# Second-layer weights with eight neighbouring rows on a partition, and ScalarE writing the first layer's result in that order

## The chip, the cores and the metric

The kernel runs on one core of a Trainium2 chip. The metric is the device time of one execution in microseconds, taken as the median of several runs. Five engines matter here: TensorE (PE, with its weight loads as PEld), VectorE (DVE), ScalarE (ACT), GpSimd (POOL) and SyncE (SP). The last two also start most of the DMA transfers.

## What is computed

A linear attention with cosine weights over 8 batches of 576 tokens is followed by a mixture of experts with one expert per token. The change is in the experts, whose core is

```python
def _moe_ref(x, w_gate, w_output_gate, w1, w2):          # x: 4608 x 512
    e_idx = np.argmax(x @ w_gate, axis=1)                # 8 experts
    ...
    for e in range(E):
        mask = e_idx == e
        h = np.maximum(x[mask] @ w1[e], 0.0)             # w1[e]: 512 x 1024
        ye = h @ w2[e]                                   # w2[e]: 1024 x 512
        out[mask] = gate_w[mask, None] * eom[mask, e, None] * ye
```

The weights are float32 in memory; the kernel turns them into float16 while they are loaded.

## The kernel before

The program has two stages that overlap a little. Up to about 159 us the attention is computed batch by batch in 36 units (a batch and a pair of token chunks), whose finished rows are scattered, sorted by expert, into a buffer in memory (`xs`). From then on the experts' work is done in tiles of 128 sorted rows, 39 of them in the main loop, numbered j.

The order of instructions on each engine is the order in which the code is written. A tile passes through these steps: `fetch(j)` loads its rows from `xs`; `x_tr(j)` transposes them on TensorE (tile `xtsp`) and ScalarE copies the result out (`xts`, line 801); `layer1(j)` runs 8 matmuls of 512 columns into `hp`, 1024 float32 values on each partition (line 836), and ScalarE takes the positive part of them and writes it as float16 into `hs` (line 845, for tile 0 in two halves, line 848); `h_tr(j)` transposes `hs` in 8 blocks of 128 columns, on TensorE (line 818) with a VectorE copy into `hts` (line 820), or, for the tiles 18 to 36 (`BY_DMA`), by a DMA transpose that SyncE starts (line 813); `layer2(j)` runs 8 matmuls of 512 columns into `yp` (line 868), VectorE scales the result, and GpSimd scatters it into the output (line 879).

In the main loop TensorE's order for a tile outside `BY_DMA` is

```python
            if j < NMAIN and j - 1 not in BY_DMA:
                h_tr(j - 1)
            if j + 1 < NMAIN:
                x_tr(j + 1)
            ...
                layer1(j)
            ...
                    layer2(m)      # m = j - 1; m = j - 2 where m is in BY_DMA
```

so that the 8 matmuls of one `layer2` stand between the end of `layer1(j)` and the first transpose of `hs(j)`.

The weights of the 8 experts are loaded by GpSimd in order of rank, two DMAs for each: `load_w(r, 0)` brings the first layer (line 238), `load_w(r, 1)` the second (line 241). They are started between the scatters of rows and of results, all on GpSimd's one DMA queue. ScalarE waits on the semaphores of the loads (`wsem`) ahead of the copy of line 801.

Of the kernel before, what the change touches and what calls it, by code (L numbers as in the profile page):

```python
# [17 lines left out]
AF = mybir.ActivationFunctionType  # L18
# [4 lines left out]
def kernel(  # L23
# [13 lines left out]
    ACT = nc.scalar  # L37
# [191 lines left out]
    def load_w(r, m):  # L229

        if r not in wreg:
            wreg[r] = GP.value_load(ordi[0:1, r:r + 1], min_val=0, max_val=E - 1)
            if r > 1:

                GP.wait_ge(wsem[r % 2], 16 * (r % 2) + 32 * (r // 2))
        er = wreg[r]
        if m == 0:
            d = GP.dma_start(w1v[:, r], moe_w1[bass.ds(er, 1)].rearrange(
                "o (c p) f -> p (o c) f", p=128))
        else:  # L240
            d = GP.dma_start(w2v[:, r], moe_w2[bass.ds(er, 1)].rearrange(
                "o (c p) d2 -> p (o c) d2", p=128))
        d.then_inc(wsem[r % 2], 16)
        tc.declare_no_dep(d.ins, group="mm", reason="ranks loaded before")
        tc.add_to_no_dep_group("w", d.ins)
# [28 lines left out]
    if True:  # L274
# [488 lines left out]
        def tcol(m, j):  # L763
            tab, jj = (tabs[0], j) if j < EARLY else (tabs[1], j - EARLY)
            return tab[jj:jj + 1, m:m + 1]
# [56 lines left out]
        def layer1(j, hp_t=None):  # L822
            ev = PE.value_load(tcol(2, j), min_val=0, max_val=7)
            evr[j] = ev
            xts = xtss.pop(j)
            hs = fsb.tile([P, F], F16, name=f"hs{j}", tag="hs", bufs=3)
            hss[j] = hs
            if hp_t is None:
                hp_t = pqo.tile([P, 4, 256], F32, name=f"hp{j}", tag="qo")
                hp = hp_t[:].rearrange("p a w -> p (a w)")  # L830
                hps = [hp[:, 0:512], hp[:, 512:1024]]
            else:
                hp, hps = None, [x[:] for x in hp_t]
            for fh in range(2):
                for kc in range(4):
                    mm = PE.matmul(hps[fh], xts[:, kc, :],  # L836
                                   wt[:, bass.ds(ev, 1),
                                      kc * F + fh * 512:kc * F + fh * 512 + 512],
                                   start=(kc == 0), stop=(kc == 3))
                    tc.declare_no_dep(mm.ins, group="w", reason="waits on wsem")  # L840
                    tc.add_to_no_dep_group("mm", mm.ins)
                    if j < 2:
                        tc.declare_no_dep(mm.ins, group="att", reason="is of rank 0 or 1")
            if hp is not None:
                ACT.activation(hs[:], hp, AF.Relu)  # L845
            else:
                for fh in range(2):
                    ACT.activation(hs[:, fh * 512:fh * 512 + 512], hps[fh], AF.Relu)

        spare = {}  # L850

# [131 lines left out]
        for i, (b, c) in enumerate(units):  # L983
# [86 lines left out]
            for w in wload.get(i, ()):  # L1070
                load_w(*w)
# [5 lines left out]
        rows = []  # L1077
        q_out(*outs[0], late=rows)
        layer1(0, kv_tiles("hp"))
        x_tr(2)  # L1080
        layer1(1)
        h_tr(0)
        next(first_half, None)
        scatter(NG - 1, 0)
        scatter(NG - 1, 1)
        q_out(*outs[1], late=rows)
        load_w(3, 1)
        layer1(2)
        h_tr(1)
        x_tr(3)  # L1090
# [16 lines left out]
        next(late)  # L1107
        layer2(2)
        load_w(4, 1)
        for j in range(4, NMAIN + 1):  # L1110
            if j < NMAIN and j - 1 not in BY_DMA:
# [67 lines left out]
```

## Time and profile before

| | us |
|---|---|
| median of 3 runs | 329.62 |
| the three runs | 331.42, 329.14, 329.62 |
| profiled execution, its own time | 331.24 |
| its span from the first to the last instruction | 329.4 |

The profile is of one execution. Its time is 1.84 us longer than its span. TensorE has a matmul under way in 284.5 us of the span (86%), VectorE is busy for 179.0 us, ScalarE for 176.7 us and GpSimd for 134.0 us. Each expert's first-layer weights are 512 rows of 4 KB in memory, the second-layer weights 1024 rows of 2 KB; half as many bytes arrive on chip, because they are turned into float16 on the way.

### The profile page before, as it was taken

How to read it: one execution, taken by the hardware profiler on the slowest of the kernel's cores; microseconds unless marked ns; L12 is line 12 of the kernel's file. 1: busy time of each engine (PE TensorE's matmuls, PEld its weight loads, DVE VectorE, ACT ScalarE, POOL GpSimd, SP SyncE). 2: the span in 40 equal slices, each digit the busy share in tenths (PEclk: the TensorE clock that was granted, in tenths of full speed). 3: DMA queues.
4: the chain of work that ended last, by engine and by line, in shares of the span. 5: the costliest groups of instructions: out<-in, count | busy, mean ns of one | idle time of the engine just before them, and what ended most of it. 6: DMA issues, size and time to landing. Idle time of an engine off the chain costs nothing. (4 is left out here: it accounts for less than half of the span.)

```text
span 329.4 us, 10190 instructions
## 1 busy us (share of the span) xinstructions
PE 284.5 (86%) x3624; PEld 180.3 (55%) x3624; DVE 179.0 (54%) x534; ACT 176.7 (54%) x346; POOL 134.0 (41%) x169
## 2 busy tenths in 40 slices
PE   6888898997887769787982989999999999999990
PEld 2566687775776557654541455555554444444440
DVE  7347688877989987967681633333322222322240
ACT  4488899887787658835620323333345344444410
POOL 8002224358625676388267343252221322232231
PEclk9999999999999989979998799999999999999997
DMA  7999779686956899999977999999948867785711
GB/s 245 339 385 334 188 241 310 209 288 245 315 170 216 242 241 259 220 221 252 217 123 223 159 232 234 233 240 255 284 89 196 184 169 190 176 183 137 193 46 46
DMA packets 58208, 71.87 MB, mean 218 GB/s; under 512 B 23406, under 2 KB 38318, under 8 KB 58160
## 3 DMA queue, kind: packets, MB, share of 16 engines
q0 software_dynamic: 17552, 31.05, 42.5%
q1 hardware_dynamic: 40608, 40.17, 41.6%
q8 instruction: 32, 0.52, 0.7%
q14 instruction: 16, 0.13, 0.1%
HBM read 67.61 MB, written 16.17 MB: 254 GB/s over the span
## 5 line engine op out<-in xcount | busy, mean ns | idle before, releaser
L868 PE MATMUL yp<-wt,hts 128*128 x312 | 75.1, 385 | 6.7 <-issue 6.7
L836 PE MATMUL hp<-wt,xts 128*128 x304 | 71.8, 379 | 0.5 <-issue 0.4
L536 POOL TENSOR_TENSOR xr<-wt,rc 128x512 f16<-128x512 f32 x33 | 37.3, 1139 | 61.6 <-DVE rc L547 53.7
L845 ACT ACTIVATE hs<-hp 128x1024 f16<-128x1024 f32 x38 | 38.9, 1023 | 39.7 <-PE hp L836 39.7
L875 DVE TENSOR_SCALAR ysp<-yp,xg 128x512 f32<-128x512 f32 x24 | 18.0, 751 | 69.0 <-PE yp L868 69.0
L868 PEld LDWEIGHTS <-hts 128*128 128x128 f16 x312 | 30.7, 99 | 43.9 <-issue 8.8
L521 PE MATMUL qo<-kvm,wt 64*64 64x162 f32 x1024 | 44.3, 304 | 9.8 <-DVE rc L546 5.1
L801 ACT COPY xts<-xtsp 128x512 f16<-128x512 f16 x39 | 22.7, 586 | 51.0 <-PE xtsp L785 37.3
L526 ACT ACTIVATE wt<-qo,cosq 128x324 f32<-128x324 f32 x72 | 36.0, 531 | 23.4 <-PE qo L521 18.1
L528 DVE SCALAR_TENSOR_TENSOR wt<-qo,sinq,wt 128x324 f32<-128x324 f32 x72 | 37.3, 550 | 19.9 <-ACT wt L526 16.3
L836 PEld LDWEIGHTS <-xts 128*128 128x128 f16 x312 | 29.1, 98 | 29.3 <-issue 1.3
L384 PE MATMUL kvp<-wt 64*64 64x132 f32 x1152 | 40.6, 278 | 4.7 <-issue 1.9
L521 PEld LDWEIGHTS qo<-kvm,wt 64*64 64x64 f32 x1024 | 35.1, 133 | 14.8 <-DVE wt L528 6.3
L384 PEld LDWEIGHTS kvp<-wt 64*64 64x64 f32 x1152 | 32.5, 132 | 9.9 <-issue 5.2
L879 POOL DMA_INDIRECT out_dram<-ysp,sidx x17 | 16.7, 985 | 48.3 <-DVE sidx L805 40.3
L336 ACT ACTIVATE wt<-wt,tanc 128x256 f32<-128x256 f32 x63 | 28.5, 516 | 0.0
L875 DVE TENSOR_SCALAR ysb<-yp,xg 128x512 f32<-128x512 f32 x15 | 11.3, 751 | 28.9 <-PE yp L868 26.8
L342 DVE TENSOR_SCALAR wt<-wt,cosc 128x256 f32<-128x256 f32 x63 | 24.4, 434 | 0.0
L498 PE MATMUL qtp<-ident,qr 128*128 128x128 f32 x128 | 21.8, 295 | 1.5 <-ACT qr L486 1.0
L879 POOL DMA_INDIRECT out_dram<-ysb,sidx x11 | 10.8, 984 | 28.2 <-DVE ysb L875 16.7
L486 ACT ACTIVATE qr<-wt 128x512 f32<-128x512 f32 x32 | 20.6, 648 | 0.0
L501 ACT COPY wt<-qtp 128x512 f32<-128x512 f32 x32 | 18.9, 591 | 1.6 <-PE qtp L498 1.1
(274 smaller groups left out, 322.7 us busy)
## 6 DMA issues: line engine op xcount, KB each, us to landing
wt<-in_moe_w_dram POOLq DMA_DIRECT2D x16, 1024.0 KB
wt<-in_k_dram SPq DMA_DIRECT2D x16, 576.0 KB
wt<-in_v_dram SPq DMA_DIRECT2D x16, 576.0 KB
wt<-in_q_dram SPq DMA_DIRECT2D x16, 576.0 KB
xg<-xs SPq DMA_DIRECT2D x43, 129.0 KB
xs<-zt SPq DMA_DIRECT2D x9, 129.0 KB
hts<-hs SPq DMA_TRANSPOSE x19
out_dram<-ysp,sidx POOLq DMA_INDIRECT x17
```

The lines of the kernel that those rows point to most:

```text
L336: d = ACT.activation(tvs[:, c, :, 1:65], vbuf[b % 2][:, :, c, :], AF.Copy, scale=tanc[:, c:c + 1])
L342: DVE.tensor_scalar(kcs[:, :, c, :], kbuf[b % 2][:, :, c, :], cosc[:, c:c + 1], 0.0, ALU.mult, ALU.max)
L384: mm = PE.matmul(outs(i, mp), kcs[rows, m, c, :], mov, start=first, stop=(c == NCH - 1), skip_group_check=True)
L521: PE.matmul(qo[64 * l:64 * l + 64, 2 * mp + ih, 0:162], qT[r, hf, ih, l, :], kvms[b if c < 4 else b - 1 + l][r, n0:n0 + 2, :], start=True, ...
L526: d0 = ACT.activation(t, qo[:, :, 0:81], AF.Copy, scale=cosq[:, c:c + 1])
L528: d1 = DVE.scalar_tensor_tensor(u[:, h0:h0 + 4, :], qo[:, :, 81:162], sinq[:, c:c + 1], t, ALU.mult, ALU.add)
L536: e.tensor_tensor(xrows[:, slot + x, 0:DM].bitcast(F16).rearrange("p (h d) -> p h d", d=D), u[:, 8 * x:8 * x + 8, 0:64], rc[:, 8 * x:8 * x ...
L836: mm = PE.matmul(hps[fh], xts[:, kc, :], wt[:, bass.ds(ev, 1), kc * F + fh * 512:kc * F + fh * 512 + 512], start=(kc == 0), stop=(kc == 3))
L845: ACT.activation(hs[:], hp, AF.Relu)
L868: mm = PE.matmul(yp, hts[:, fc, :], wt[:, bass.ds(ev, 1), 4 * F + fc * DM:4 * F + fc * DM + DM], start=(fc == 0), stop=(fc == 7))
L875: DVE.tensor_scalar(ysb, yp, xg[:, DM + 2:DM + 4].bitcast(F32), None, ALU.mult)
L879: d = GP.indirect_dma_start(out=out[:, :], out_offset=bass.IndirectOffsetOnAxis(ap=idx, axis=0), in_=ysb, in_offset=None, bounds_check=N - ...
```

## The change

Before, partition p gets the rows p, 128 + p, 256 + p, ... of the second-layer weights: eight pieces of 2 KB from eight places. Afterwards it gets the rows 8p to 8p + 7, which are neighbours: 16 KB from one place. The second layer then multiplies, in its step c, the features 8p + c instead of 128c + p. So the 128 columns of block c of `hs` must hold the features c, 8 + c, 16 + c, ..., and ScalarE reads every eighth value of `hp` for each block: its input steps by 32 bytes through the accumulator memory (PSUM), where it read neighbours before. Its output is written in order as before. For tile 0 each half writes 64 columns of each block.

```diff
         else:
             d = GP.dma_start(w2v[:, r], moe_w2[bass.ds(er, 1)].rearrange(
-                "o (c p) d2 -> p (o c) d2", p=128))
+                "o (p c) d2 -> p (o c) d2", p=128))
...
+            hv = hs[:].rearrange("p (c q) -> p c q", c=8)
             if hp is not None:
-                ACT.activation(hs[:], hp, AF.Relu)
+                ACT.activation(hv, hp.rearrange("p (q c) -> p c q", c=8), AF.Relu)
             else:
                 for fh in range(2):
-                    ACT.activation(hs[:, fh * 512:fh * 512 + 512], hps[fh], AF.Relu)
+                    ACT.activation(hv[:, :, fh * 64:fh * 64 + 64],
+                                   hps[fh].rearrange("p (q c) -> p c q", c=8), AF.Relu)
```

No instruction moves. On GpSimd, around the load of the first expert's second-layer weights, the program of before has this order (`xs` are scattered rows, `xr` the rows in the making, 128x8x512 the shape of the load):

```order
L238 DMA wt<-in_moe_w_dram 128x4x1024
L633 DMA xs<-xr_1014,di@1_0_1852 36992x516
L536 TENSOR_TENSOR xr_1643<-wt,rc_4_2082 128x512
L633 DMA xs<-xr_1014,di@1_0_1852 36992x516
L536 TENSOR_TENSOR xr_1643<-wt,rc_4_2082 128x512
L241 DMA wt<-in_moe_w_dram 128x8x512
```

The changed program has the same order there:

```order
L238 DMA wt<-in_moe_w_dram 128x4x1024
L633 DMA xs<-xr_1014,di@1_0_1852 36992x516
L536 TENSOR_TENSOR xr_1643<-wt,rc_4_2082 128x512
L633 DMA xs<-xr_1014,di@1_0_1852 36992x516
L536 TENSOR_TENSOR xr_1643<-wt,rc_4_2082 128x512
L241 DMA wt<-in_moe_w_dram 128x4096
```

Only the shape of the load differs: one run of 4096 values for a partition in place of eight runs of 512.

## Rows read from the trace of the kernel before

**Rows 1.** Busy time by stretch: engines, granted clock, DMA share, GB/s.

```profile
core 0: us, PE busy (x) PEld busy (x) DVE busy (x) ACT busy (x) POOL busy (x), PEclk, DMA share, GB/s
200.00:210.00 10.00, 10.00 (x65) 5.30 (x64) 3.44 (x7) 3.80 (x5) 4.79 (x5) 1.00 1.16 233
260.00:280.00 20.00, 20.00 (x110) 9.69 (x109) 4.37 (x10) 9.06 (x11) 4.99 (x6) 1.00 0.73 180
```

**Rows 2.** Timeline of PE, 199 to 213 us: start, us, what.

```profile
201.47 1.89 PE L868 MATMUL yp<-wt,hts 128*128 x8
203.20 0.61 PE L818 MATMUL htsp<-ident,hs 128*128 128x128 f16 x8
203.64 0.39 PE L785 MATMUL xtsp<-ident,xg 128*128 128x128 f16 x4
203.87 1.89 PE L836 MATMUL hp<-wt,xts 128*128 x8
205.59 1.89 PE L868 MATMUL yp<-wt,hts 128*128 x8
207.32 0.61 PE L818 MATMUL htsp<-ident,hs 128*128 128x128 f16 x8
```

**Rows 3.** Timeline of ACT, the same stretch.

```profile
201.67 1.02 ACT L845 ACTIVATE hs<-hp 128x1024 f16<-128x1024 f32 x1 [1.06 <-PE hp L836]
204.14 0.58 ACT L801 COPY xts<-xtsp 128x512 f16<-128x512 f16 x1 [1.45 <-PE xtsp L785]
205.79 1.02 ACT L845 ACTIVATE hs<-hp 128x1024 f16<-128x1024 f32 x1 [1.06 <-PE hp L836]
```

**Rows 4.** Timeline of PE's weight loads, 206 to 209 us.

```profile
207.11 0.65 PEld L818 LDWEIGHTS <-hs 128*128 128x128 f16 x8
```

**Rows 5.** Timeline of all engines, 183.5 to 185.4 us.

```profile
183.85 1.03 ACT L845 ACTIVATE hs<-hp 128x1024 f16<-128x1024 f32 x1
184.93 0.10 PEld L818 LDWEIGHTS <-hs 128*128 128x128 f16 x1 [0.34 <-ACT hs L845]
```

**Rows 6.** Groups by line and shape: count, busy us, mean ns, idle before.

```profile
L845 ACT ACTIVATE hs<-hp 128x1024 f16<-128x1024 f32 x38 | 38.9, 1023 | 39.7 <-PE hp L836 39.7
L848 ACT ACTIVATE hs<-kvphp 128x512 f16<-128x512 f32 x2 | 1.1, 593 | 0.0
L558 DVE TENSOR_REDUCE glog<-gl 128x32 f32<-128x256 f32 x16 | 9.5, 592 | 0.5
L558 DVE TENSOR_REDUCE glog<-gl 128x16 f32<-128x128 f32 x4 | 1.5, 368 | 0.1
```

**Rows 7.** Line 581, a reduction over neighbouring values: ns minimum/median/maximum.

```profile
L581 DVE TENSOR_REDUCE ei@0_0_1056<-oh@0_0_1053 x1: 230/230/230, 57.4 to 57.4; 128x9 f32<-128x72 f32 x1
...
L581 DVE TENSOR_REDUCE ei@3_0_2764<-oh@3_0_2761 x1: 186/186/186, 145.2 to 145.2; 128x4 f32<-128x32 f32 x1
```

**Rows 8.** Line 845 from 183.8 to 243 us.

```profile
L845 ACT ACTIVATE hs<-hp x14: 1023/1023/1030, 183.9 to 239.0; 128x1024 f16<-128x1024 f32 x14
```

**Rows 9.** Timeline of ACT, 310 to 321.5 us: the last two tiles.

```profile
311.49 1.02 ACT L845 ACTIVATE hs<-hp 128x1024 f16<-128x1024 f32 x1 [1.09 <-PE hp L836]
315.44 1.02 ACT L845 ACTIVATE hs<-hp 128x1024 f16<-128x1024 f32 x1 [2.93 <-PE hp L836]
```

**Rows 10.** Who waited for whom, PE's weight loads, 184 to 322 us.

```profile
PEld L868 <- DMA hts<-hs: 0.2, 1, 0.2
```

**Rows 11.** DMA packets from 207 to 209 us: a second-layer load fills the queue.

```profile
DMA packets 408, 0.42 MB, mean 211 GB/s; under 512 B 2, under 2 KB 406, under 8 KB 408
```

**Rows 12.** DMA packets from 213 to 215 us: a first-layer load fills the queue.

```profile
DMA packets 210, 0.43 MB, mean 215 GB/s; under 512 B 2, under 2 KB 2, under 8 KB 210
```

**Rows 13.** The weights in memory: who starts their loads, and who waited.

```profile
L238 POOL DMA_DIRECT2D wt<-in_moe_w_dram x8: 798/806/837, 109.4 to 213.6; - x8
...
L241 POOL DMA_DIRECT2D wt<-in_moe_w_dram x8: 952/974/1000, 116.4 to 217.9; - x8
...
  ACT xts L801: 1.4, 1
```

**Rows 14.** Timeline of ACT, 223 to 232 us, around that one wait.

```profile
224.92 0.58 ACT L801 COPY xts<-xtsp 128x512 f16<-128x512 f16 x1 [1.45 <-PE xtsp L785]
...
229.04 0.59 ACT L801 COPY xts<-xtsp 128x512 f16<-128x512 f16 x1 [1.45 <-DMA wt<-in_moe_w_dram]
```

**Rows 15.** Waits of POOL and then of PE, 100 to 160 us: total, times, longest.

```profile
POOL xr L536 <- DMA xs<-xr,di@1_0_1852: 7.7, 1, 7.7
...
PE qo L521 <- DVE wt L528: 5.1, 6, 1.8
PE qo L521 <- DVE rc L546: 3.1, 2, 1.7
```

## The prediction

> **What bounds the kernel now.** I began with the busy time by stretch. [...] The view of the chain that ended last holds two pieces here, both in the last 8 us, and is of no use. Next came the timelines of PE and ACT side by side for one tile. Outside the DMA-transposed tiles, TensorE's period is 4.12 us (first transpose of `hs` at 203.20, the next at 207.32) [rows 2], and inside it ScalarE's step on `hs` starts at 205.79 and lasts 1.02 us [rows 3]. The reader is to see how narrow the gap is. The weight load of the first transpose starts at 207.11 [rows 4]. The one place where it had to wait for `hs` shows the delay between the two: the step ended at 183.85 + 1.03 = 184.88, the load started at 184.93 [rows 5], 0.05 us later. So the slack is 207.11 - (205.79 + 1.02) - 0.05 = 0.25 us a tile. All that ScalarE's step grows beyond that, TensorE waits for.
>
> **What the load gains.** Both loads already run near one rate. In 2 us in which a second-layer load fills the queue, 408 packets bring 0.42 MB, 211 GB/s, nearly all of them the 1 KB that a 2 KB row becomes [rows 11]; in 2 us of a first-layer load, whose pieces are twice as long, 210 packets bring 0.43 MB, 215 GB/s [rows 12]. A piece twice as long was worth 2%. A load of 1 MB takes some 5.0 us at 211 GB/s, so 0.1 us each if eight-fold pieces gain as much again as two-fold ones did, and 0.3 us if each doubling does (three doublings, 6%). For the four loads of ranks 0 to 3, which go out while attention and the first tiles run, that is 0.4 to 1.2 us. On GpSimd the start of a second-layer load takes 0.97 us against 0.81 for a first-layer load with half the pieces [rows 13]; with an eighth of the pieces I expect it below 0.81, eight times 0.2 to 0.3 us, beside TensorE's work.
>
> Who would notice? In the experts' stage nobody: the one wait ended by a weight load is the copy at 229.04, and it was idle for 1.45 us before it, exactly as the copy at 224.92 was while waiting for TensorE [rows 14], so the load landed as the transposes did. In the attention, GpSimd waited once, 7.7 us, for scattered rows that stand in the same queue behind weight loads, and TensorE waited for VectorE for 5.1 and 3.1 us in that stretch [rows 15]. One second-layer load, of rank 0, lies ahead of those rows; so 0.1 to 0.3 us of that wait can go. I take -0.3 us for all of this. The other bound is a loss: a piece eight times as long holds a DMA engine eight times as long, and the query loads and instruction fetches that share the engines wait behind it. The trace shows no such piece in a queue of weights. I allow up to +1 us there, a fifth of the 5 us for which one weight load holds the engines, and use it for the range only.
>
> **What ScalarE's step costs.** No row shows ScalarE reading PSUM with a step. So I bound it. Below: the cost is nothing; the step stays at 1023 ns [rows 6]. A gain has no source, since the number of values, the output and the count of instructions are the same. Above: the nearest row is VectorE's reduction of line 558, which reads float32 values 64 bytes apart (in SBUF, not PSUM). 256 values take 592 ns and 128 take 368 [rows 6], so 224/128 = 1.75 ns a value. A reduction over neighbours takes 230 ns for 72 values and 186 for 32 [rows 7], 44/40 = 1.10 ns a value. The step made each value 1.6 times as dear. ScalarE's own price for neighbours: 1024 values 1023 ns, 512 values 593 ns [rows 6], so 0.84 ns a value and 163 ns fixed. With the factor 1.6 its step becomes 163 + 1024 x 1.34 = 1.54 us; with VectorE's 1.75 ns outright it becomes 1.95 us; a doubled price, if each value needs an access of its own where two neighbours shared one, gives 163 + 1024 x 1.68 = 1.88 us. I take 1.88 us, growth 0.86 us, because the row's price of 1.75 ns is an access time that should bind whichever engine reads, and it is nearly twice ScalarE's 0.84.
>
> That rows of another memory decide this is the weak step. [...]
>
> **The sum.** Growth 0.86 us less slack 0.25 us is 0.61 us for a tile whose transposes follow one `layer2` behind. From tile 4 on there are 14 such tiles before the DMA transposes begin [rows 8], and the last two, which have the same order around them [rows 9]: 16 x 0.61 = 9.8 us. Tiles 0 to 3 have other work between, and cost nothing. In the tiles 18 to 36 the transposed block is used two tiles later; only one load of weights waited for a DMA transpose at all, 0.2 us [rows 10], that of tile 18, the first. It has no slack, and I charge it 0.6 us. The others have two periods of 3.7 us ahead of them, and ScalarE at 45% [rows 1] becomes 70%: enough. Behind ScalarE's longer step its copy of line 801 is queued, but that waits 1.45 us for TensorE now [rows 3], and moves with it. So +9.8 + 0.6 - 0.3 = +10.1 us on the profiled execution's 331.24, that is 341.3; the median of the runs is 1.6 us lower, so **339.7 us**, 3.1% slower. With a factor of 1.6 (1.54 us; growth 0.52, exposed 0.27) it is 16 x 0.27 + 0.3 - 0.3 = +4.3, 333.9 us; with 1.95 us, +11.2, 340.8 us.
>
> **The rivals.** *ScalarE does not care.* PSUM may hand out a value a cycle whatever the step; TensorE writes 8 times 512 columns into it between 203.87 and 205.59 us [rows 2], 0.42 ns a value, so the memory is faster than ScalarE's 0.84 ns by a factor of two, and half its rate would still feed ScalarE. Then only the load's -0.3 us is left: 329.3 us, no change. The condition is a step at most 0.25 us longer than now. [...] I find this nearly as likely as the forecast. *The queue relaxes.* If the attention stage's wait of GpSimd [rows 15] falls by half, 3.8 us, because the rows behind the load land sooner than the rates say, and ScalarE does not care either, TensorE's 8.2 us of waits for VectorE fall with it, to 326 us. The 2% between the two packet sizes speaks against it. *The pieces are not merged.* The built program holds one run of 4096 values, but the DMA may cut it again; then the packets stay at 1 KB and the load's -0.3 us goes, nothing else.
>
> **How the numbers follow.** A change of 1% is about what a measurement of this kernel can tell from none. Forecast (step 1.7 to 1.95 us, 336.5 to 341.5): 0.46. A smaller penalty (1.3 to 1.7 us, 330 to 336): 0.06, most of it slower than 1%, above 332.9. ScalarE does not care (327.8 to 331.5): 0.40. The queue relaxes: 0.08. Slower 0.51, same 0.41, faster 0.08. The range runs over both large cases, from 327.8 to 341.8. The forecast's own range is 336.5 to 341.5.
>
> **What would show it.** Line 846 of the changed kernel (845 before): some 1.88 us right, 1.02 us wrong. The period between the transposes of `hs` around 200 us: 4.7 against 4.12 us, with the weight load waiting for `hs` each time, where one did before. Between 245 and 310 us the period should stay at 3.7 us. Packets of the second-layer loads: fewer and longer, the rate in their stretches 211 to 225 GB/s. The start of these loads on GpSimd: below 0.81 us. The forecast fails if the step costs ScalarE nothing, or if the longer pieces delay the query loads by more than a microsecond.

## The result, and the profile after

The changed kernel took 319.8 us (median of 5 runs, 317.56 to 321.71) against 329.62 us before (5 runs, 327.37 to 331.42): a ratio of 0.970, 95% interval 0.963 to 0.978. The forecast was 339.7 us. On another chip, with 6 and 18 runs, the medians were 323.2 and 328.9 us, ratio 0.980 (0.973 to 0.988). Ratios leave out the slower executions of either kernel, medians don't; single executions of one kernel spread over 10 us, so a median of 6 to 12 of them is good to some 2 us.

The forecast rested on ScalarE's step. Groups by line and shape, changed kernel (lines moved by one or two; 846 was 845):

```profile
L846 ACT ACTIVATE hs<-hp 128x1024 f16<-128x1024 f32 x38 | 38.9, 1024 | 40.8 <-PE hp L836 40.8
L849 ACT ACTIVATE hs<-kvphp 128x512 f16<-128x512 f32 x2 | 1.2, 597 | 1.2 <-PE kvphp L836 1.2
```

1024 ns against 1023 [rows 6]: reading PSUM in steps of 32 bytes cost ScalarE nothing. So the experts' stage keeps its pace; the transposes of `hs` follow each other after 4.13 us, as after 4.12 in [rows 2]. Timeline of PE:

```profile
199.04 0.61 PE L818 MATMUL htsp<-ident,hs 128*128 128x128 f16 x8
...
203.17 0.61 PE L818 MATMUL htsp<-ident,hs 128*128 128x128 f16 x8
```

Busy time by stretch, as [rows 1]:

```profile
200.00:210.00 10.00, 10.00 (x66) 5.26 (x65) 3.66 (x8) 3.91 (x6) 2.23 (x4) 1.00 1.06 230
260.00:280.00 20.00, 20.00 (x110) 9.69 (x108) 4.37 (x10) 8.97 (x11) 5.69 (x6) 1.00 0.77 176
```

A matmul is under way in 10.00 of 10.00 and 20.00 of 20.00 us, at a granted clock of 1.00, while ScalarE is busy for 39% and 45%, much as in [rows 1]: in these stretches TensorE sets the time, and another engine matters where it makes TensorE wait.

GpSimd's start of a second-layer load fell from 974 to 618 ns [rows 13], beside other work. Duration of one, minimum, median, maximum:

```profile
L241 POOL DMA_DIRECT2D wt<-in_moe_w_dram x8: 577/618/642, 116.0 to 210.8; - x8
```

In the attention the waits of GpSimd and TensorE are little changed, 8.2 us for 7.7 (put down to VectorE now, no longer to the scattered rows) and 3.8 + 3.4 for 5.1 + 3.1 [rows 15]. Waits of POOL and PE, 100 to 160 us:

```profile
POOL xr L536 <- DVE ds@2_0_2563 L609: 8.2, 1, 8.2
...
PE qo L521 <- DVE wt L528: 3.8, 4, 1.4
PE qo L521 <- DVE rc L546: 3.4, 2, 1.9
```

Where did the time come from, then? The trace of before that the rows stand for has a wait which its second trace, taken later, does not have (below). That second trace (326.67 us, span 324.8) is the one to hold against the changed kernel's (318.74 us, span 316.9). The two are level where the change begins to act: the first packet of a weight load moves at 112.5 and 112.8 us. In the 18 traces of all the kernels here this point lies anywhere from 112.3 to 119.9 us, so much of the spread of single executions arises ahead of anything that the change touches. Timeline of PE around tile 18, the first whose transpose is done by DMA; the second trace of before:

```profile
230.78 1.89 PE L868 MATMUL yp<-wt,hts 128*128 x8
...
235.10 1.89 PE L836 MATMUL hp<-wt,xts 128*128 x8
242.11 3.57 PE L868 MATMUL yp<-wt,hts 128*128 x8 [5.12 <-DMA hts<-hs]
...
247.90 1.89 PE L868 MATMUL yp<-wt,hts 128*128 x8
...
251.58 0.59 PE L868 MATMUL yp<-wt,hts 128*128 x2
```

The changed kernel:

```profile
230.46 1.89 PE L870 MATMUL yp<-wt,hts 128*128 x8
...
234.46 1.89 PE L836 MATMUL hp<-wt,xts 128*128 x8
238.44 1.89 PE L870 MATMUL yp<-wt,hts 128*128 x8 [2.08 <-DMA hts<-hs]
...
242.11 1.89 PE L870 MATMUL yp<-wt,hts 128*128 x8
...
245.79 1.89 PE L870 MATMUL yp<-wt,hts 128*128 x8
```

Up to `layer2` of tile 17 the two are level (230.78 and 230.46, 0.3 us). Tile 18 begins at 242.11 against 238.44: 3.4 us more apart, 3.0 of them in the wait itself (5.1 and 2.1 us). After the long wait the eight matmuls take 3.57 us instead of 1.89, because the granted clock fell from 1.00 to 0.50 while TensorE waited: it is 0.50 in each microsecond from 240 to 246. The same was seen with a shorter wait: the changed kernel kept 1.00 after its 2.1 us, e1 (below) fell to 0.50 with a wait as long and took 3.54 us. Busy time by stretch of the second trace of before, then of the changed kernel:

```profile
240.00:250.00 10.00, 7.89 (x33) 3.70 (x34) 1.04 (x3) 1.61 (x2) 0.98 (x1) 0.68 0.50 135
```

```profile
240.00:250.00 10.00, 10.00 (x57) 4.93 (x56) 2.62 (x6) 4.14 (x6) 2.95 (x3) 1.00 0.66 163
```

0.68 against 1.00; by tile 20 the distance is 5.8 us (251.58 and 245.79), 2.1 us more. It stays 5.8 us to GpSimd's last scatter. The last row of POOL's timeline, second trace of before and changed kernel:

```profile
317.48 0.98 POOL L879 DMA_INDIRECT out_dram<-ysb,sidx  x1 [0.74 <-DVEq L1136]
```

```profile
311.69 0.98 POOL L881 DMA_INDIRECT out_dram<-ysb,sidx  x1 [0.74 <-DVEq L1138]
```

From there to the end of the span it is 324.83 - 318.46 = 6.37 us before and 316.91 - 312.67 = 4.24 us now: 2.1 us more. So 7.9 us = 0.3 (all up to tile 17) + 3.4 (up to the start of tile 18, nearly all of it the wait) + 2.1 (the half clock behind it) + 2.1 (the end). That is the split of one pair of executions. The changed kernel's second trace has a span of 324.5 us, with a first weight packet at 116.6 and a wait of 3.9 us; counted from the first weight packet to the end of the span, the three take 212.4 (before), 204.1 and 207.9 us.

Why tile 18? All weight loads from rank 4 on leave GpSimd's queue in one row, with scatters between them. DMA packets from 190 to 230 us and the weights' queue, second trace of before:

```profile
DMA packets 6369, 9.59 MB, mean 240 GB/s; under 512 B 304, under 2 KB 4023, under 8 KB 6364
...
q0 software_dynamic: 5500, 8.73, 108.0%
```

The changed kernel:

```profile
DMA packets 3939, 9.98 MB, mean 250 GB/s; under 512 B 350, under 2 KB 1242, under 8 KB 3550
...
q0 software_dynamic: 2929, 8.99, 99.3%
```

The 16 DMA engines are full with that one queue (108% and 99% of them). The single packet records of the traces say the rest. A packet of 1 KB took 98 ns, one of 2 KB 173 (medians, first trace of before), one of 8 KB 625 (changed kernel). From those records, in us:

```
trace                       A      B     C     D     wait
before, second trace        44.9   8.0   7.7   1.6   5.1
ScalarE's step alone (e2)   44.7   8.1   7.7   0.8   4.3
early ranks alone (e3)      44.8   8.5   7.6   1.7   4.9
reversed rows (e5)          44.6   7.8   5.7   0.6   1.9
late ranks alone (e4)       44.2   6.4   6.4   0.6   0.6
load alone (e1)             44.1   6.8   7.6   0.8   2.1
changed kernel              44.2   6.4   7.4   1.1   2.1
changed kernel, second      44.1   6.4   7.1   3.0   3.9
A  from the first packet of the first second-layer load of ranks 4 to 7 to that of the last
B  the last load, from its first packet to the end of its last
C  from there to the end of the packets of tile 18's transposed block
D  from there to the start of layer2(18)
wait  TensorE's wait for that block, by the view of waits
```

In A lie seven loads, 6.3 to 6.4 us each in either layout, as the near equal rates of [rows 11] and [rows 12] say; but with 8 KB pieces the last load was through in 6.4 to 6.8 us and not in 7.8 to 8.5 (B). Between two loads that is hidden, since the next one already runs. Behind the last it is not: five fetches of rows, five scatters and then the transposed block of tile 18 stand there and need some 7 us more (C, 5.7 to 7.7). The wait does not follow B alone: e5 waited only 1.9 us with 1 KB pieces, its C being the shortest, and the changed kernel's second trace 3.9 us with 8 KB pieces, its D being 3.0 and its late loads beginning later. What sets C and D stays open.

### The profile page after: what moved, and what is told of

It is laid out like the page before. It is cut to its first block, busy times and chain, and to the rows that moved or that the text cites. A ratio compares the mean times of both kernels' runs of the same rounds, so it can differ in the third digit from the quotient of the medians.

```text
span 316.9 us, 10190 instructions
## 1 busy us (share of the span) xinstructions
PE 280.4 (88%) x3624; PEld 178.7 (56%) x3624; DVE 178.2 (56%) x534; ACT 177.5 (56%) x346; POOL 130.9 (41%) x169
## 3 DMA queue, kind: packets, MB, share of 16 engines
q0 software_dynamic: 10384, 31.05, 40.6%
## 5 line engine op out<-in xcount | busy, mean ns | idle before, releaser
L870 PE MATMUL yp<-wt,hts 128*128 x312 | 73.4, 379 | 2.1 <-DMA hts<-hs 2.1
L846 ACT ACTIVATE hs<-hp 128x1024 f16<-128x1024 f32 x38 | 38.9, 1024 | 40.8 <-PE hp L836 40.8
L521 PE MATMUL qo<-kvm,wt 64*64 64x162 f32 x1024 | 43.5, 300 | 9.4 <-DVE rc L546 5.4
L881 POOL DMA_INDIRECT out_dram<-ysp,sidx x17 | 16.8, 986 | 48.7 <-DVE sidx L805 42.6
L877 DVE TENSOR_SCALAR ysb<-yp,xg 128x512 f32<-128x512 f32 x15 | 11.3, 750 | 26.6 <-PE yp L870 26.6
L498 PE MATMUL qtp<-ident,qr 128*128 128x128 f32 x128 | 21.0, 287 | 1.5 <-ACT qr L486 1.0
```

What stands on the lines that cost most here:

```text
L521: PE.matmul(qo[64 * l:64 * l + 64, 2 * mp + ih, 0:162], qT[r, hf, ih, l, :], kvms[b if c < 4 else b - 1 + l][r, n0:n0 + 2, :], start=True, ...
L846: ACT.activation(hv, hp.rearrange("p (q c) -> p c q", c=8), AF.Relu)
L870: mm = PE.matmul(yp, hts[:, fc, :], wt[:, bass.ds(ev, 1), 4 * F + fc * DM:4 * F + fc * DM + DM], start=(fc == 0), stop=(fc == 7))
L877: DVE.tensor_scalar(ysb, yp, xg[:, DM + 2:DM + 4].bitcast(F32), None, ALU.mult)
L881: d = GP.indirect_dma_start(out=out[:, :], out_offset=bass.IndirectOffsetOnAxis(ap=idx, axis=0), in_=ysb, in_offset=None, bounds_check=N - ...
```

## The experiments

The first four ask which part of the change brings the gain, and theory A in them is only that the longer pieces do, the early ones (A1) or the late ones (A2). From the second group on theory A is the one above: the end of the last load holds up tile 18. The differences given in us are of medians.

Medians in us, of all runs, with the kernel before on the same chip:

```
                                   median  runs  before  ratio (95%)
e1  load alone                     320.9    6    328.3   0.981 (0.965 to 0.996)
e2  ScalarE's step alone           328.5   12    328.3   0.994 (0.985 to 1.002)
e3  ranks 0 to 3 alone             329.0    6    328.3   1.012 (1.002 to 1.023)
e4  ranks 4 to 7 alone             322.6   12    328.3   0.990 (0.981 to 0.999)
    changed kernel                 323.2    6    328.9   0.980 (0.973 to 0.988)
e8  before, DMA from tile 20       323.5    7    328.9   0.986 (0.981 to 0.991)
e9  changed, DMA from tile 20      319.8    6    328.9   0.976 (0.971 to 0.982)
e6  both layers                    328.4   12    328.9   1.000 (0.996 to 1.003)
e13 last rank alone                325.5   12    328.6   0.993 (0.987 to 1.000)
e5  rows in reverse                326.7   12    328.6   1.000 (0.995 to 1.005)
e7  two rows in place of eight     323.8   12    328.6   0.988 (0.982 to 0.994)
```

**Which half of the change, and which loads?** The load alone:

```diff
-                "o (c p) d2 -> p (o c) d2", p=128))
+                "o (p c) d2 -> p (o c) d2", p=128))
```

> The load alone in the new layout; ScalarE writes its result in the old order, so the second layer pairs features with the wrong rows of weights and the output is not the reference's. Theory A (the longer pieces give the whole gain, and ScalarE's strided read costs nothing): as fast as the changed kernel, 318 to 321.5 us, ratio 0.97. Rival B (the strided read does cost a little that the traces hide): faster than the changed kernel by 2 us or more, below 317 us. Rival C (the gain needs both, or is a shift in the timing of the program that any edit could cause): between 323 and 330 us.

ScalarE's order alone:

```diff
+                ACT.activation(hv, hp.rearrange("p (q c) -> p c q", c=8), AF.Relu)
```

> ScalarE's strided read alone, with the old layout of the load; the second layer pairs features with the wrong rows, so the output is not the reference's. Theory A (only the load matters): 328 to 331 us, ratio 0.995 to 1.005, the step on hs 1023 ns. The prediction's own step (the read costs 0.86 us a tile, 0.61 us of it in the open): 339.7 us, ratio 1.03. Rival C (any edit moves the stall): below 326 us.

The load alone brings 7.4 us, ScalarE's order alone nothing (its step on `hs` 1023 ns). The gain is the load's.

```diff
+                "o (p c) d2 -> p (o c) d2" if r < 4 else "o (c p) d2 -> p (o c) d2", p=128))
```

> ScalarE as in the changed kernel; the new layout for the second-layer loads of ranks 0 to 3 alone, which go out during the attention and up to 166 us; ranks 4 to 7 are loaded as before, so their tiles pair features with the wrong rows and the output is not the reference's. Theory A1 (the gain comes in the attention and at the start of the experts' stage, where loads share the DMA queues with everything else): 319 to 322 us. Rival A2 (it comes from the later loads, in the experts' stage): 328 to 331 us. If both halves matter: some 325 us.

```diff
+                "o (p c) d2 -> p (o c) d2" if r >= 4 else "o (c p) d2 -> p (o c) d2", p=128))
```

> The counterpart: the new layout for ranks 4 to 7 alone (loads issued after 185 us), ranks 0 to 3 as before, whose tiles pair features with the wrong rows, so the output is not the reference's. Theory A1: 327 to 330.5 us, ratio 0.99 to 1.00, and the stall of TensorE between 173 and 185 us is there. Rival A2: 319 to 322 us.

I had expected the early loads to matter, in the attention. They don't: 329.0 us, while the late ranks alone bring 5.7 us (1.0% by the ratio, its interval ending just under 1). That theory (A1) fell, and the wait at tile 18 came into view: 4.9 us in e3, 0.6 us in e4.

**Is it the wait at tile 18?** The first two kernels move the DMA transposes away from the end of the loads; the third makes the first layer's pieces longer too.

> The changed kernel itself, for its times and a second trace beside the next three kernels. Theory A (the end of the last weight load, and the backlog of fetched rows and scatters behind it, decides when the first DMA transpose of hs can run; shorter second-layer loads bring that end forward): 318 to 323 us, the last load ends 50 us after the first load of the experts' stage, and the second layer of tile 18 begins 8 to 9 us after that end. Rival B (the 11 us of waiting between 173 and 185 us in the trace of before are what the change removes): 318 to 323 us too, and no such wait.

```diff
-    BY_DMA = range(18, 37)
+    BY_DMA = range(20, 37)
```

> The kernel before, with the DMA transposes of hs beginning at tile 20 instead of tile 18, so that tiles 18 and 19 are transposed on TensorE (2 x 0.45 us more work there) and nothing waits for the DMA queue while the last weight loads run. Theory A: the wait at tile 18 (4 to 7 us with the half clock behind it, in the traces with the old layout of the late ranks) goes, 323 to 325 us. Rival B: the wait lies elsewhere, so 328 to 330 us.

> The changed kernel, with the DMA transposes beginning at tile 20. Theory A: the changed kernel's own wait at tile 18 (2 to 4 us) goes against 0.9 us more on TensorE: 317 to 319 us; and the distance to the same edit of the kernel before shrinks from some 8 us to 5 us or less. Rival B: the distance to the same edit of the kernel before stays at 8 us or more.

In the kernel before, the edit brings 5.4 us although TensorE does some 0.9 us more (an estimate: two tiles at 4.12 us in place of 3.68); in the changed one 3.4 us (319.8 us, a little above the 317 to 319 expected); and the distance between the two kernels shrinks from 5.7 to 3.7 us, by the ratios from 2.0% to 1.0%. Medians good to 2 us would not show that alone; the traces do, in which tile 18 has no wait. e9 has the lowest median on its chip, 9.1 us under the kernel before. PE's timeline of e9 shows tile 18 without a wait, 4.12 us after tile 17:

```profile
230.72 1.89 PE L870 MATMUL yp<-wt,hts 128*128 x8
...
234.84 1.89 PE L870 MATMUL yp<-wt,hts 128*128 x8
...
238.97 1.89 PE L870 MATMUL yp<-wt,hts 128*128 x8
```

The changed kernel's second trace waited 3.9 us there, longer than I expected: its late loads began 26.5 us after its first matmul into `hp` (24.3 us in the first trace), so the loads ended later for TensorE.

```diff
-                "o (c p) f -> p (o c) f", p=128))
+                "o (p c) f -> p (o c) f", p=128))
...
-                             xg[:, kc * 128:(kc + 1) * 128].bitcast(F16), ident16[:, :])
+                             xg[:, kc:512:4].bitcast(F16), ident16[:, :])
```

> The changed kernel with the first layer's weights also in neighbouring rows, four on a partition, and the transposes of the fetched rows reading every fourth column to match. Theory A: the last load ends another 1 to 3 us earlier and the wait at tile 18 shrinks by as much: 317 to 319 us. Rival B: no effect, 319 to 322 us. If TensorE reads columns 8 bytes apart more slowly, 39 x 4 transposes show it, and it is slower.

The wait at tile 18 is 0.3 us there, as expected, and the kernel still lost: 5.2 us slower than the changed one. The strided transposes are not why: 219 ns each, as before, and 113 ns in place of 98 for the weight load beside each. Two things are. From the first weight packet to the first matmul into `hp` it took 44.4 us against 40.7 and 40.9 in the traces of the changed kernel and of e9 from the same chip; and the end grew. The last row of POOL's timeline, in a span of 328.04 us:

```profile
316.40 0.98 POOL L881 DMA_INDIRECT out_dram<-ysb,sidx  x1 [0.75 <-DVEq L1138]
```

That leaves 328.04 - 317.38 = 10.7 us behind it, where the changed kernel has 4.2.

**The last load, the size of the pieces, and the wait of the first trace.**

```diff
+                "o (p c) d2 -> p (o c) d2" if r == 7 else "o (c p) d2 -> p (o c) d2", p=128))
```

> ScalarE as in the changed kernel, and the new layout for the second-layer load of the last rank, 7, alone; the tiles of the other ranks pair features with the wrong rows, so the output is not the reference's. Theory A in its sharper form (the loads follow each other 6.1 us apart in either layout; what the layout shortens is the time from the first packet of a load to its last, 8.8 to 6 us, and that counts for the last load, behind which the fetched rows, the scatters and the first DMA transposes wait): the last load takes 6 us, tile 18 begins 8 to 9 us behind its end, and the time is 3 to 4 us under the kernel before, 324 to 326 us. If each of the late loads gives its share, it is 1 to 1.5 us under it, 327 to 328 us.

3.1 us from one load of eight, inside the expected range; but the interval of the ratio reaches 1.000, so the times alone do not tell it from no gain. Its trace shows the mechanism, if less of it than the expectation asked: the last load took 7.0 us, not 6, and TensorE waited 0.8 us at tile 18.

```diff
+            d = GP.dma_start(w2v[:, r, ::-1], moe_w2[bass.ds(er, 1)].rearrange(
...
+            hv = hs[:].rearrange("p (c q) -> p c q", c=8)[:, ::-1]
```

> The same eight neighbouring rows on each partition, but laid down there in reverse order, so that no two of them can be one piece; ScalarE's columns in the same reverse order. Theory A (the size of the pieces decides): as many packets as before (17552 in the queue), each second-layer load 8 to 8.8 us from its first packet to its last, and the time of the kernel before, 327 to 330 us. Rival (neighbouring addresses in memory decide): 320 to 323 us with the loads at 6 us.

326.7 us with 17552 packets, ratio 1.000: it is the size of a piece, not the neighbourhood of the addresses. Loads took 7.6 to 8.8 us. (The median is 1.9 us under the kernel before, about what the medians can tell.)

```diff
+            d = GP.dma_start(w2v[:, r].rearrange("p (h l) d2 -> p h (l d2)", l=2),
+                moe_w2[bass.ds(er, 1)].rearrange(
+                    "o (h p l) d2 -> p (o h) (l d2)", p=128, l=2))
```

> Two neighbouring rows on a partition instead of eight, with ScalarE's columns to match: pieces twice as long as before, as the first layer's are. Theory A: a second-layer load takes some 7.3 us from its first packet to its last, as first-layer loads do, so the last one ends 1.5 us earlier than in the kernel before: 325 to 327 us. If only the eight-fold piece helps: 328 to 330 us; if the first doubling gives nearly everything: 320 to 323 us.

4.8 us, more than expected (ratio 0.988). The changed kernel was not measured on this chip; beside its 5.7 and 9.8 us on two others, the first doubling gives half of the gain or more.

> A second trace of the kernel before. Theory A: the 11 us of waiting between 173 and 185 us are not in every execution; where they are missing, TensorE waits for 4 to 8 us at tile 18 for its DMA transpose instead, and the span is 323 to 330 us either way. Rival B: the wait at 173 to 185 us is there again.

The second trace of before has no wait between 173 and 185 us. The rows of that wait, PE's timeline of the first trace:

```profile
173.31 1.89 PE L836 MATMUL hp<-wt,xts 128*128 x8
181.93 3.57 PE L868 MATMUL yp<-wt,hts 128*128 x8 [6.73 <-issue]
```

and the same place in t3 (below), whose second-layer loads are all in the new layout:

```profile
173.79 1.89 PE L836 MATMUL hp<-wt,xts 128*128 x8
180.23 3.25 PE L870 MATMUL yp<-wt,hts 128*128 x8 [4.55 <-issue]
```

It comes in some executions with either layout (5 of the 18 traces), so the change does not remove it; what starts it, and whether the change makes it rarer, stays open. What it does is to make TensorE late: in the first trace of before tile 18 began at 248.6, 11.3 us after the last load's end, and found its block ready but for 0.2 us [rows 10].

**What the end depends on.** One execution of each, on a further chip, where the kernel before took 337.7 us.

```diff
+                "o (p c) d2 -> p (o c) d2" if r < 6 else "o (c p) d2 -> p (o c) d2", p=128))
```

> The new layout for the second-layer loads of ranks 0 to 5 alone, 12176 packets in the weights' queue; the tiles of ranks 6 and 7 pair features with the wrong rows, so the output is not the reference's. From the end of GpSimd's last scatter to the end of the span: about 5.2 us if that stretch goes steadily with the number of packets, 6.1 or 4.2 us if in steps. The last load is in the old layout, so it takes 7.5 to 8.8 us from its first packet to its last and the wait at tile 18 is there, 4 to 8 us: span 321 to 328 us.

```diff
+                "o (p c) f -> p (o c) f" if r == 7 else "o (c p) f -> p (o c) f", p=128))
```

> The changed kernel with the first layer's weights of rank 7 in neighbouring rows as well, 10000 packets; the tiles of that rank pair features with the wrong rows, so the output is not the reference's. The end stretch: some 4.0 us if it goes with the number of packets down to here; 10 us if one first-layer load in this form brings the long one of the kernel with both layers.

```diff
+                "o (p c) f -> p (o c) f" if r > 3 else "o (c p) f -> p (o c) f", p=128))
```

> The changed kernel with the first layer's weights of ranks 4 to 7 in neighbouring rows as well, 8848 packets; the tiles of those ranks pair features with the wrong rows, so the output is not the reference's. The end stretch: 3 to 4 us if it falls with the number of packets, 7 us if it rises steadily from 10384 to 7312, 10.6 us if it is a step. The attention loads as in the changed kernel, so the first layer of tile 0 begins 40 to 43 us after the first weight load, not the 44.4 us of both layers.

> Both layers in neighbouring rows and the DMA transposes from tile 20, 7312 packets. The end stretch: 10.6 us again if it belongs to the number of packets, 4 us if it was one execution's. The wait at tile 18 is gone; the first layer of tile 0 begins some 44 us after the first weight load. Span 324 to 328 us.

They took 335.7, 337.7, 330.5 and 339.6 us. From the end of GpSimd's last scatter to the end of the span, with all traces:

```
packets in the weights' queue   17552  16656  13968  13456  12176  10384  10000   8848   7312
end stretch, us                   6.4    6.4    6.1    6.1    5.9    4.2    4.2    4.2   10.7
```

Traces with the same number agree within 0.1 us, whatever ranks were changed and whatever went before (e11 repeats e6's 10.7 us). So it goes with the number of packets, in steps and not in one direction, though t1's 5.9 us was none of the values expected. t2 and t3 held the 4.2 us of the changed kernel; the long one comes between 8848 and 7312 packets, where the first-layer pieces of ranks 0 to 3 changed as well, and no run parts the two. The records show GpSimd in one drain instruction for most of it (4.48 us before, 2.77 changed, 7.91 with both layers); what it drains stays open. All four traces had the intermittent wait ahead of `layer2` of tile 3, so TensorE reached tile 18 some 12 to 16 us after the last load's end and waited 0.5 us at most; and the spans of t1 and e11, 333.8 and 338.0 us, came out above the 328 us that were expected at most. t2, nearly the changed kernel, took 337.74 us against 337.7 before: where that wait comes, the gain at tile 18 is not there to be had. That is one execution of each.

## Why the prediction was wrong

**The step that failed** is the price of ScalarE's step: "I take 1.88 us, growth 0.86 us, because the row's price of 1.75 ns is an access time that should bind whichever engine reads". A price of VectorE reading SBUF was carried over to ScalarE reading PSUM. The growth was 0.001 us, and the 16 x 0.61 us and the 0.6 us at tile 18 went with it; e2, with that read alone, cost nothing. The 1.88 us were reckoned from a doubled price of a value, an assumption of mine; no run shows such a price, or two neighbours sharing an access: the step took 1024 ns (1023 in e2). The slack of 0.25 us a tile was never touched and stays untested.

**The rival named the step, not the time.** "ScalarE does not care" gave 329.3 us, 9.5 too many, because a second step failed: "In the experts' stage nobody" notices a load that lands sooner. That came from [rows 10] and [rows 14], which are true of an execution in which TensorE was late by the intermittent wait. A trace in which an engine was held up cannot show that a transfer behind it is hidden. In executions without it, TensorE waited 4.3 to 5.1 us for tile 18's block in the old layout of the late ranks (1.9 in e5) and 0.6 to 3.9 us in the new one.

**The load's gain was read from the wrong measure.** The rates of [rows 11] and [rows 12] were right, and with them the spacing of the loads: the seven loads of A, three of them of the second layer, became 0.7 us shorter (44.9 to 44.2), within the "0.1 to 0.3 us each". But a rate in the middle of a load says nothing of its end, and the last load's end came 1.6 us earlier (B). Together 2.3 us; tile 18 began 3.4 us sooner (C and D, 0.8 us shorter too, are in it), and the clock made it 5.5.

**"The queue relaxes"** came nearest, 326 us with a chance of 0.08: the mechanism (rows behind a load land sooner than the rates say) was right, the place was not the attention. There, from the first weight packet to the first matmul into `hp`, all traces but the last four give 40.7 to 43.0 us where the early second-layer loads alone come in 8 KB pieces and 42.6 to 45.9 where they come in 1 KB; e3's time does not show it, and in the last four it was 42.9 to 47.6 with the new layout. In one trace transfers of another engine waited while a load ran out: of the five fetches that SP started from 226.72 on in the second trace of before, the first packet moved at 230.2, 3.5 us later (GpSimd's last load ended at 232.8); for a fetch started at 255.47 there, with no load under way, it took 1.5 us.

**Right:** GpSimd's start of a load below 0.81 us (0.618) with nobody to notice; the period of 3.7 us behind tile 18 (238.44, 242.11, 245.79). **Not in the sum:** the end stretch, -2.1 us. **The allowance of 1 us for long pieces** that hold up others was not needed for the second layer; an 8 KB packet took 6.4 times as long as one of 1 KB (625 and 98 ns), not eight times, and what was seen to wait behind a load were fetches of rows (3.5 us, above); with both layers long one trace shows 3.7 us (44.4 against 40.7).

**The sum as the runs show it.** By the pair of traces 7.9 us. By medians on the chip of e8 and e9 5.7 us: moving the transposes is worth 5.4 + 0.9 us before and 3.4 + 0.9 us after, so 2.0 us are the wait at tile 18 and its clock; 2.1 us are the end; 1.6 us remain, which the attention may hold but no run proves. Of these terms only the end repeats to 0.1 us; the others are estimates from medians good to some 2 us. On the first chip it was 9.8 us; what made it more there stays open.

## What to carry to other kernels

Take a transfer's cost from its first packet to its last and ask what stands behind the last of a row; a rate in the middle says nothing of that. Before a wait is called hidden, look whether the engine was late for another reason in the traced execution, and take a second trace. Hold two executions together from the first instruction that the change touches, not from their start. A price carried from another engine and another memory is a bound, not a value to choose.

## What the runs showed of the hardware

- ScalarE read float32 from PSUM in steps of 32 bytes as fast as neighbours: 1024 ns (changed kernel) and 1023 ns (before) for 1024 values.
- TensorE transposed columns 8 bytes apart in SBUF at 219 ns each (e6), as it did neighbours (before); the weight load took 113 ns for 98.
- A packet of a converting weight load took 98, 173 and 625 ns for 1, 2 and 8 KB, yet loads followed each other 6.3 to 6.4 us apart in either layout; the size showed in how long the last load took, 6.4 us in the changed kernel and 8.0 in the second trace of before.
- GpSimd's last stretch went with how many packets its queue moved: 6.4 us at 17552 (before), 4.2 at 10384 (changed kernel), 10.7 at 7312 (e6, e11).
